# A linear-attention and mixture-of-experts kernel: attention in plain fp32 on halves of the matmul array, and expert units whose second layer lags and whose end is shared

## The chip, the cores and the metric

The kernel runs on one core of a Trainium2 chip. The metric is the device time of one launch in microseconds; lower is better. A core has a matmul engine (TensorE, PE in the profile, its weight loads PEld), a vector engine (VectorE, DVE), a scalar engine (ScalarE, ACT), GpSimd (POOL) and a synchronisation engine (SyncE, SP) that issues most of the transfers. PE writes into PSUM, 8 banks of 128 partitions x 512 fp32; everything else stands in SBUF or in device memory.

## The reference

Attention with exponential features, then one expert per token:

```
def phi(x):
    proj = einsum('bhsd,df->bhsf', x, w_phi)              # 64 -> 128
    proj = proj - max(abs(proj), axis=-1, keepdims=True)
    return concatenate([exp(proj), exp(-proj)], axis=-1)  # 256 features
q_p, k_p = phi(q), phi(k)
kv  = einsum('bhsf,bhsd->bhfd', k_p, v);  z = sum(k_p, axis=2)
attn = einsum('bhsf,bhfd->bhsd', q_p, kv) / (einsum('bhsf,bhf->bhs', q_p, z) + 1e-6)

x = attn as (4608, 512)
xn, en = x and expert_emb, each row divided by (its norm + 1e-6)
logits = xn @ en.T / tau;  expert = argmax(logits);  gate = softmax(logits)[expert]
out[token] = gate * (relu(x[token] @ w1[expert]) @ w2[expert])   # 512 -> 1024 -> 512
```

The shapes are 8 batches, 8 heads, 576 tokens and 64 columns a head; 8 experts; all arrays are fp32.

## The kernel before, in words

**Attention** goes through 16 quads: one quad is two pairs of heads (X = 0, 1; e = 0, 1 within a pair) of half a batch. `load` and `load_v` (L174, L182) bring q, k and v of a quad. Each of them is split into two float32r parts, the rounded value and what the rounding leaves: `split`, `split_v` and `split_k` (L208, L215, L244) do it with a copy on ACT or DVE (L203, L206) and a subtraction on DVE or POOL (L197). A product of two such pairs is three float32r matmuls, high by high, high by low and low by high.

A quad has nine blocks of 128 tokens in five groups (`GR`: 2, 2, 1, 2, 2 blocks). `proj` (L220) multiplies a group of q or k by the features: per block three matmuls at L229, 128 x 256 results for both heads of a pair at once, by a weight matrix that holds w_phi twice on its diagonal. Then DVE takes the largest absolute value of each row out of PSUM (L233) and subtracts it (L235). For keys, ACT makes the two exponentials (L242); for queries, PE transposes the blocks (`qtr`, L257) and ACT makes the exponentials from PSUM (L260). `kv` (L269) forms [v 1]^T k_p with 65 weight columns and 256 moving columns, three matmuls per block (L282), and ACT copies it (L285). `kve` (L287) turns it around on PE (L296), which also multiplies it with the experts' normalised embeddings, so that every head has 73 columns: 64 of kv, the sum, and 8 dots with the embeddings. DVE copies them (L298). `num` (L303) multiplies the queries' features by these in plain fp32 (L310, L313), and `norm` (L316) divides on DVE and writes x, and each fourth time sends x to device memory. `frame` (L844) writes out the order of a quad's work by hand, with the routing steps of earlier tokens put between (`pop`, `square`). On PE this order is kept; the other engines are ordered by a scheduler. The first quad is `first_frame` (L927), in written order on all engines but SP.

**Routing** (`route`, `early`, `tables`; L381, L466, L489) computes experts and gates on DVE and puts the tokens into a table by expert with indirect transfers of POOL. `tables` then makes a list of units: an expert's tokens in slots of 128, two slots to a unit; where the number of slots is odd, an expert has a first unit of three slots (the third may hold 32, 64 or 96 tokens), or a single one.

**Experts.** Unit 0 has three slots and begins before routing is through. Every later unit is a switch (L838) with 12 arms: 6 sizes, each with or without being an expert's last. Each arm holds the whole unit (`unit`, L799). In `layers` (L718) chunk c of the hidden features (128 of 1024) goes through layer 1: 12 matmuls (L688), weights w1 in halves, tokens moving; ACT makes the rounded part (L690) and DVE the rest (L693). Then comes layer 2 of chunk c - 1: per slot three matmuls with 512 moving columns (L711, L706). Layer 1 uses two PSUM banks in turn, and the hidden features three buffers. In an expert's last unit the next expert's weights are split chunk by chunk (`next_w1`, `next_w2`, L584). POOL gathers the rows of a unit two ahead (L604), DVE transposes the next unit's (L617), and ACT and DVE split them (`xsplit`, L641) into the one pair of buffers xh, xl. A unit of one slot has code of its own (`layers_of_slot`, L750), in which w1 moves (L765) and the hidden features are turned by PE (L774). A unit ends with ACT multiplying by the gate (L817) and POOL writing the rows out by an indirect transfer (L823).

## Time and profile before

| what | us |
|---|---|
| three runs, median (lowest to highest) | 1093.22 (1090.64 to 1102.72) |
| span of the one profiled execution, whose own time the page gives only as this span | 1133.1 |
| PE busy in it | 965.3 (85%) |
| DVE busy | 651.2 (57%) |
| POOL busy | 538.0 (47%) |
| ACT busy | 433.5 (38%) |
| mean granted PE clock | 0.908 of full speed |

The profiled execution is longer than the runs, and its rows add up to its own span. A row of instructions in order of time has the start, the duration, engine, line, operation, result<-operands and shape; in brackets the idle time ahead of it and what ended that. A row of groups has the count, the busy time, the mean duration in ns, and after the second bar the idle time ahead. Matmuls overlap: the time from one start to the next is the price of one, and its duration is longer. In "128\*64 128x73" the first pair is the weights' rows and columns, the second the moving operand. float32r shows as f32 there.

### The profile page before, as it was taken

How to read it: one execution, taken by the hardware profiler on the slowest of the kernel's cores; microseconds unless marked ns; L12 is line 12 of the kernel's file. 1: busy time of each engine (PE TensorE's matmuls, PEld its weight loads, DVE VectorE, ACT ScalarE, POOL GpSimd, SP SyncE). 2: the span in 40 equal slices, each digit the busy share in tenths (PEclk: the TensorE clock that was granted, in tenths of full speed). 3: DMA queues.
4: the chain of work that ended last, by engine and by line, in shares of the span. 5: the costliest groups of instructions: out<-in, count | busy, mean ns of one | idle time of the engine just before them, and what ended most of it. 6: DMA issues, size and time to landing. Idle time of an engine off the chain costs nothing. (4 is left out here: it accounts for less than half of the span.)

```text
span 1133.1 us, 17328 instructions
## 1 busy us (share of the span) xinstructions
PE 965.3 (85%) x6188; PEld 860.1 (76%) x6188; DVE 651.2 (57%) x1289; ACT 433.5 (38%) x841; POOL 538.0 (47%) x396
## 2 busy tenths in 40 slices
PE   6999999999899989988898788698687588798874
PEld 4899888888788878877787677587576477687763
DVE  8888898989899898969221223324225623422221
ACT  5556554645354554543221223314225413312221
POOL 5555564776477664655433224325144454422322
PEclk7999998999899999989899888799788778899887
DMA  5223221313132224111611111514313531511111
GB/s 166 83 66 106 61 88 46 105 51 106 63 105 66 79 90 180 45 29 43 215 37 49 38 40 49 191 23 126 106 45 116 159 123 46 188 28 45 47 35 43
DMA packets 55822, 94.22 MB, mean 83 GB/s; under 512 B 22471, under 2 KB 22855, under 8 KB 55440
## 3 DMA queue, kind: packets, MB, share of 16 engines
q1 hardware_dynamic: 45808, 68.97, 19.2%
q0 software_dynamic: 9632, 21.32, 6.3%
q14 instruction: 285, 2.33, 0.7%
q8 instruction: 97, 1.59, 0.7%
HBM read 70.64 MB, written 19.96 MB: 80 GB/s over the span
## 5 line engine op out<-in xcount | busy, mean ns | idle before, releaser
L604 POOL DMA_INDIRECT xg<-xd,ix x156 | 152.6, 978 | 260.2 <-DVE xt L617 168.5
L693 DVE SCALAR_TENSOR_TENSOR hl<-bk,hh 128x256 fp32r<-128x256 f32 (+2 forms) x128 | 57.6, 452 | 340.9 <-ACT hh L690 275.9
L197 POOL TENSOR_TENSOR kpl<-kp,kph 128x1024 fp32r<-128x1024 f32 (+1 forms) x79 | 170.1, 2153 | 121.3 <-DVE kph L206 111.7
L688 PE MATMUL bk<-xh,w1h 128*128 128x256 f32 (+4 forms) x512 | 169.5, 331 | 61.6 <-issue 54.2
L690 ACT ACTIVATE hh<-bk 128x256 fp32r<-128x256 f32 (+4 forms) x128 | 52.6, 415 | 346.4 <-PE bk L688 248.7
L688 PEld LDWEIGHTS bk<-xh,w1h 128*128 128x128 f32 x512 | 111.2, 217 | 73.4 <-issue 60.7
L688 PE MATMUL bk<-xl,w1h 128*128 128x256 f32 (+4 forms) x512 | 166.6, 325 | 0.0
L688 PE MATMUL bk<-xh,w1l 128*128 128x256 f32 (+4 forms) x512 | 165.9, 324 | 0.0
L260 ACT ACTIVATE qp<-bk 128x512 f32<-128x512 f32 (+1 forms) x160 | 79.9, 552 | 148.0 <-PE bk L257 134.5
L310 PE MATMUL np<-kvs,qp 128*128 128x73 f32 x992 | 126.1, 283 | 0.0
L310 PEld LDWEIGHTS np<-kvs,qp 128*128 128x128 f32 x992 | 124.2, 203 | 0.1
L688 PEld LDWEIGHTS bk<-xl,w1h 128*128 128x128 f32 x512 | 111.7, 218 | 4.9
L233 DVE TENSOR_REDUCE m<-bk 128x4 f32<-128x512 f32 (+1 forms) x157 | 98.9, 632 | 28.4 <-PE bk L229 22.6
L206 DVE CAST kph<-kp 128x1024 fp32r<-128x1024 f32 (+1 forms) x77 | 109.7, 1424 | 6.6 <-ACT kp L242 6.1
L688 PEld LDWEIGHTS bk<-xh,w1l 128*128 128x128 f32 x512 | 110.9, 217 | 0.0
L242 ACT ACTIVATE kp<-kd 128x512 f32<-128x512 f32 (+1 forms) x160 | 83.6, 580 | 50.2 <-DVE kd L235 49.5
L823 POOL DMA_INDIRECT out<-o,ent x39 | 41.0, 1052 | 95.5 <-ACT o L817 88.6
L711 PE MATMUL bk<-w2h,hh 128*128 128x512 f32 x136 | 59.7, 439 | 31.2 <-ACT hh L690 23.2
L711 PE MATMUL np<-w2h,hl 128*128 128x512 f32 (+1 forms) x160 | 65.7, 411 | 0.0
L711 PE MATMUL np<-w2h,hh 128*128 128x512 f32 (+1 forms) x160 | 65.4, 409 | 0.0
L711 PE MATMUL np<-w2l,hh 128*128 128x512 f32 (+1 forms) x160 | 65.2, 408 | 0.0
L257 PE MATMUL bk<-cst,qd 128*128 128x128 f32 x288 | 50.3, 296 | 8.9 <-DVE qd L235 8.9
(248 smaller groups left out, 2210.6 us busy)
## 6 DMA issues: line engine op xcount, KB each, us to landing
w1r<-w SPq DMA_DIRECT2D x14, 1024.0 KB
w2r<-w SPq DMA_DIRECT2D x14, 1024.0 KB
q<-qT SPq DMA_DIRECT2D x16, 576.0 KB
k<-kT SPq DMA_DIRECT2D x15, 576.0 KB
xd<-x SPq DMA_DIRECT2D x8, 1024.0 KB
va<-va SPq DMA_DIRECT2D x16, 325.0 KB
va<-va SPq DMA_DIRECT2D x16, 260.0 KB
xg<-xd,ix POOLq DMA_INDIRECT x156
```

Of the source, the lines that this page charges most:

```text
L197: ins = eng.tensor_tensor(out=hl[1], in0=raw, in1=hl[0].bitcast(F32), op=ALU.subtract)
L206: self.v.tensor_copy(out=out, in_=in_)
L233: v.tensor_reduce(out=m, in_=pv, axis=AX.X, op=ALU.max, apply_absolute_value=True)
L242: nc.scalar.activation(out=k[:, :nu, s], in_=d[:, :nu], func=AF.Exp, scale=sc)
L257: nc.tensor.transpose(out=ps[:, e, c, :], in_=self.dq[g][:, c, e, :], identity=self.ident)
L260: nc.scalar.activation(out=q[:, s, :, :nu], in_=ps[:, :, :nu], func=AF.Exp, scale=sc)
L310: nc.tensor.matmul(out=n[:, i * W:(i + 1) * W], lhsT=self.qp[g][:, s, e, c], rhs=self.kvs[j][:, X, e, s], start=(s == 0), stop=(s == 1))
L604: ins = nc.gpsimd.indirect_dma_start(out=self.xg[i][:, q * P:(q + 1) * P], out_offset=None, in_=self.xd.rearrange("n (g d) -> (n g) d", g= ...
L688: nc.tensor.matmul(out=ps, lhsT=w[:, d, fs], rhs=x[:, d, :n], start=(d == 0 and i == 0), stop=(d == 3 and i == 2))
L690: high = nc.scalar.activation(out=hh[:, :n], in_=ps, func=AF.Relu)
L693: low = self.v.scalar_tensor_tensor(out=out, in0=ps[:, cs], scalar=0.0, in1=hh[:, cs].bitcast(F32), op0=ALU.max, op1=ALU.subtract)
L711: self.nc.tensor.matmul(out=self.acc[a // P][:b - a], lhsT=h[:, a:b], rhs=w[:, c], start=(c == 0 and i == 0), stop=(c == 7 and i == 2))
```

## The change

- **Plain fp32 instead of three float32r products.** All splits of q, k, v and of the keys' features are gone, with their buffers. `proj` multiplies each head by itself: 64 weight rows (a head's columns) at partitions 0 to 63 or 64 to 127, 128 moving columns, one matmul per block and head; the two heads' results go to the two banks of one PSUM pair, one pair for keys and one for queries.
- **kv already turned.** `kv` takes the keys' features as weights, 64 columns at a time, and [v 1 and the dots of v with the embeddings] as 73 moving columns; the result has features on the partitions, and `kve` is gone. The dots of v are made ahead by the new `vemb` from a second, transposed copy of v (vT), 8 moving columns each, and put beside v by ACT. v's array now has 10 blocks, padded by zeros, so that no block is shared.
- **num on halves.** `num` splits each block's 128 weight columns into two of 64, which write to partitions 0 to 63 and 64 to 127.
- **Five slots per quad.** The order of PE is no longer `frame` but `slot`: in each of 83 slots one group of keys, one of queries two slots later, its transposes one slot later, a quarter of kv at lag 4, and num at lags 7 and 8.
- **Experts.** The one-slot code is gone, and there are 14 arms: 2 x 7 of size, first unit of an expert, and last. Layer 2 lags layer 1 by five chunks; layer 1 uses five banks in turn, and there are eight buffers of hidden features and two pairs of token buffers. Layer 2 of the last three chunks of the first two slots, and their outputs, stand once behind the switch for all arms (`unit_end`). There the next unit's arm is read into registers and named to the engines ahead of those matmuls (`switch_hint`). The second half of w2 is split in the next expert's first unit. Instructions of one element (`idle`) give all arms the same counts. The units' order is as written on all engines.

On PE, in the steady piece of attention before (L229 proj, L310 and L313 num):

```order
L229 MATMUL bk_64<-wph,kh 128x256
L229 MATMUL bk_64<-wpl,kh 128x256
L229 MATMUL bk_64<-wph,kl 128x256
L310 MATMUL np<-kvs,qp 128x73 x8
L313 MATMUL np<-kvs,qp 64x73 x2
```

And a slot and a half of the steady piece now (L231 transposes, L243 vemb, L265 kv, L213 proj, L284 and L287 num; PE):

```order
L231 MATMUL bk_65<-cst,qd 128x128 x4
L243 MATMUL pj_63<-et,vt 128x8 x4
L265 MATMUL bk_66<-va,kp_848 64x73 x4
L265 MATMUL bk_66<-va,kp_898 64x73 x4
L265 MATMUL bk_66<-va,kp_771 64x73 x2
L265 MATMUL bk_66<-va,kp_848 64x73 x4
L265 MATMUL bk_66<-va,kp_898 64x73 x4
L265 MATMUL bk_66<-va,kp_771 64x73 x2
L213 MATMUL pj_63<-wp,kt 128x128 x2
L213 MATMUL pj_64<-wp,qt 128x128 x4
L284 MATMUL np<-kvs,qp 64x73 x16
L287 MATMUL np<-kvs,qp 64x73 x2
```

A projection of one block was three matmuls and is two, num of a head was eight of 128 rows of results and is sixteen of 64, and every row but L231 and L287 now consists of pairs on two halves.

On PE, the end of unit 0 and the switch to unit 1 before (L711 layer 2, L838 the switch, L765 the first arm):

```order
L711 MATMUL np<-w2h,hh_5534 128x512
L711 MATMUL np<-w2l,hh_5534 128x512
L711 MATMUL np<-w2h,hl_5537 128x512
L132 TENSOR_LOAD tab
L1085 SWITCH_STRIDE
L1085 ISA x2
L838 BRANCH_PREFETCH_HINT
L765 MATMUL bk_63<-w1h,xh 128x512
```

The same place now has two pieces, the first within layer 2 (L691) of unit 0, between its fifth chunk and its sixth, where the arm is read (PE):

```order
L691 MATMUL acc_5697<-w2h,qp 128x512
L691 MATMUL acc_5697<-w2l,qp 128x512
L691 MATMUL acc_5697<-w2h,qp 128x512
L140 TENSOR_LOAD tab
L714 SWITCH_STRIDE
L714 ISA
L714 BRANCH_PREFETCH_HINT
L691 MATMUL bk_66<-w2h,qp 128x512
L691 MATMUL bk_66<-w2l,qp 128x512
```

and the second, PE again, at the switch itself, 27 matmuls of layer 2 and 12 transposes later (L669 layer 1 of unit 1):

```order
L691 MATMUL acc_5697<-w2l,qp 128x512
L691 MATMUL acc_5697<-w2h,qp 128x512
L998 SWITCH_STRIDE
L998 ISA x2
L833 BRANCH_PREFETCH_HINT
L669 MATMUL pj_64<-x,w1h 128x256 x2
```

The load of the arm's number and a hint moved from directly ahead of the switch to a place with matmuls between; in later units these are the 18 of the shared end.

The core of the diff:

```diff
-NK = 5
-AT = 3, 5
-ST = 1, 3, 4
+LAG, CUT = 5, 5
+ARMS = [(k, first, last) for k, first in ((256, 0), (256, 1), (384, 1), (352, 1), (320, 1), (288, 1), (128, 1)) for last in (0, 1)]
+NB = 10
...
     def proj(self, j, n, g):
-        h, l = self.half[n]
-        self.turn += 1
-        ps = self.banks[self.turn % len(self.banks)].rearrange("p (c e f) -> p c e f", c=2, e=2)
+        ps = self.pj[1 - n][:, :, :nu]
         for c in range(nu):
             us = slice((u0 + c) * P, (u0 + c + 1) * P)
-            for i, (a, b) in enumerate(((h, self.wh), (h, self.wl), (l, self.wh))):
-                nc.tensor.matmul(out=ps[:, c].rearrange("p e f -> p (e f)"), lhsT=a[:, us], rhs=b,
-                                 start=(i == 0), stop=(i == 2))
+            for e in range(2):
+                r = slice(HD * e, HD * e + HD)
+                nc.tensor.matmul(out=ps[:, e, c], lhsT=self.raw[j, n][r, us], rhs=self.wp[r], start=True, stop=True)
...
+    def vemb(self, j, b0):
+        t = self.raw[j, 2]
+        ps = self.bk[0][:, 3 * P:], self.bk[1][:, 3 * P:]
+        for b in range(b0, b0 + 2):
+            for e in range(2):
+                r = slice(HD * e, HD * e + HD)
+                self.nc.tensor.matmul(out=ps[e][:, b * E:(b + 1) * E], lhsT=t[r, b * P:(b + 1) * P],
+                                      rhs=self.et[r, 2 * (j % 2) + b // 5], start=True, stop=True)
+        if b0 == NB - 2:
+            for e in range(2):
+                self.nc.scalar.copy(out=self.va[j][:, :, e, HD + 1:], in_=ps[e][:, :NB * E].rearrange("p (b x) -> p b x", x=E))
...
     def kv(self, j, X, e):
-            for n, (a, b) in enumerate(((vh, kh), (vl, kh), (vh, kl))):
-                nc.tensor.matmul(out=o, lhsT=a[r, u, e], rhs=b[r, c, :, e], start=(i == 0 and n == 0), stop=(i == 4 and n == 2))
+        for s in range(2):
+            c0 = (2 * e + s) * W
+            for i in range(5):
+                g, c, u = self.where(X, i) if i < 4 else (2, 0, 4)
+                for a in (0, 64):
+                    nc.tensor.matmul(out=self.bk[5][a:a + 64, c0:c0 + W], lhsT=self.kp[g][:, s, e, c, a:a + 64],
+                                     rhs=self.va[j][:, 5 * X + i, e], start=(i == 0), stop=(i == 4))
...
     def num(self, j, X, e):
             for s in range(2):
-                nc.tensor.matmul(out=n[:, i * W:(i + 1) * W], lhsT=self.qp[g][:, s, e, c], rhs=self.kvs[j][:, X, e, s],
-                                 start=(s == 0), stop=(s == 1))
+                for a in (0, 64):
+                    nc.tensor.matmul(out=n[a:a + 64, i * W:(i + 1) * W], lhsT=self.qp[g][:, s, e, c, a:a + 64], rhs=kvs[:, s],
+                                     start=(s == 0), stop=(s == 1))
...
+    def layers(self, t, n, first, e):
+        nxt = t + 1 < NU
+        slots = range(-(-n // P))
+        for c in range(8 + CUT):
+            if c < 8:
+                self.layer1(t, c, n, (8 * t + c) % 5)
+                if e is not None:
+                    self.next_w1(c, e)
...
+                if first and 1 <= c < 5:
+                    self.wsplit(1, c + 3)
...
+            if c == LAG and nxt:
+                self.ahead(t)
+            if c == 8 and nxt:
+                if e is not None:
+                    self.turned([2])
...
+                self.xtr(t + 1, 2 + (e is not None))
+            if LAG <= c < LAG + CUT:
+                self.layer2(c - LAG, n, slots)
...
+        for c in range(CUT, 8):
+            self.layer2(c, n, slots[2:])
+        if n > 2 * P:
+            self.output(t, n, 2)
...
+    def unit_end(self, t):
+        if t + 1 < NU:
+            self.arms[t + 1] = self.arm(t + 1)
+            self.tc.switch_hint(self.arms[t + 1], len(ARMS), label=f"unit{t + 1}")
+        self.done = []
+        for i in range(2):
+            for c in range(CUT, 8):
+                self.layer2(c, 2 * P, [i])
+            self.output(t, 2 * P, i)
...
-            for arm in self.tc.Switch({e: self.reg(t, 1, [e], 0, 11) for e in ENGINES}, 12):
-                self.unit(t, (P, 2 * P, 3 * P, 3 * P - 32, 3 * P - 64, 3 * P - 96)[arm // 2], arm % 2)
+            for arm in self.tc.Switch(self.arms[t], len(ARMS), hint=f"unit{t}"):
+                self.unit(t, *ARMS[arm])
+            self.unit_end(t)
             self.units(t + 1)
...
+    def slot(self, t):
+        j, r = at(-2)
+        if r is not None and j > 0:
+            self.vemb(j, 2 * r)
+        j, r = at(4, 4)
+        if j is not None:
+            self.kv(j, r // 2, r % 2)
+        j, r = at(8, 3)
+        if r in (0, 2) and not (j == NQ - 1):
+            self.num(j, r // 2, 1 - r // 2)
...
+            self.proj(j, 1, r)
+        self.square()
+        j, r = at(2)
...
+            self.proj(j, 0, r)
...
+        j, r = at(7, 4)
+        if j is not None and r in (0, 3) and not (j == NQ - 1):
+            self.num(j, r // 3, r // 3)
...
+        j, r = at(3)
+        if r is not None and not (j == NQ - 1 and r == 4):
+            self.qtr(j, r)
```

Here `at(lag)` gives the quad and the slot in it that lie `lag` slots back.

More of the change, by code (lines that the diff above doesn't have):

```diff
@@ L454, in scatter @@
                 in_=ent[:, t, :], in_offset=None)
-            for split in (self.last, self.last_k):
-                self.after(ins, split, mybir.DependencyClass.NoSync, "the splits are waited for")
             for other in self.scat:
@@ L831, in units, with first_unit, arm @@
+    def first_unit(self, extra):
+        self.done = []
+        self.first_layers(K * P, extra)
+        for i in range(K):
+            self.output(0, K * P, i)
+        self.gather_parts(2, range(2))
+    def arm(self, t):
+        return {e: self.reg(t, 1, [e], 0, len(ARMS) - 1) for e in ENGINES}
     def units(self, t):
@@ L1053, in rest @@
                 self.tables()
+                for c in range(4, 8):
+                    self.wsplit(1, c)
                 while self.sends:
```

570 lines of the change are left out of this document (201 added, 369 removed).

## The prediction

> **What bounds the kernel now.** I read the page's totals and slices first, then the busy times by stage, then the costliest groups of each stage, then the instructions in order of time at two places. The page:
>
> ```profile
> span 1133.1 us, 17328 instructions
> PE 965.3 (85%) x6188; PEld 860.1 (76%) x6188; DVE 651.2 (57%) x1289; ACT 433.5 (38%) x841; POOL 538.0 (47%) x396
> PE   6999999999899989988898788698687588798874
> DVE  8888898989899898969221223324225623422221
> PEclk7999998999899999989899888799788778899887
> ```
>
> The columns show two programs: up to slice 19 both PE and DVE are near full, after it DVE is nearly idle and PE has holes in which its clock sags. So the two are priced apart, from the table of busy times by stage (start and end, length, PE busy, PEld, DVE, ACT, POOL, granted clock, DMA share, GB/s):
>
> ```profile
> 60.00:500.00 440.00, 412.20 (x3249) 377.57 (x3247) 390.74 (x736) 226.83 (x438) 269.11 (x146) 0.97 0.26 82
> 510.10:560.50 50.40, 43.60 (x239) 38.89 (x237) 31.63 (x131) 15.51 (x34) 24.03 (x22) 0.96 0.34 109
> 560.50:1118.80 558.30, 451.65 (x2320) 393.03 (x2320) 172.74 (x327) 155.13 (x307) 206.40 (x203) 0.87 0.27 80
> 1118.80:1133.10 14.30, 0.38 (x1) 0.00 (x0) 0.00 (x0) 0.69 (x1) 2.03 (x2) 0.62 0.15 47
> ```
>
> They are a steady piece of attention, the first expert unit, units 1 to 16, and a tail without work. In attention PE is busy 94% and DVE 89%: either alone would hold the stage. The DVE groups there:
>
> ```profile
> L206 DVE CAST kph<-kp 128x1024 fp32r<-128x1024 f32 (+1 forms) x70 | 99.7, 1425 | 5.9 <-ACT kp L242 5.4
> L233 DVE TENSOR_REDUCE m<-bk 128x4 f32<-128x512 f32 (+1 forms) x141 | 88.5, 630 | 20.8 <-PE bk L229 19.9
> L197 DVE TENSOR_TENSOR ql<-q,qh 128x1152 fp32r<-128x1152 f32 x14 | 30.6, 2188 | 0.0
> L298 DVE COPY kvs<-bk 128x292 f32<-128x292 f32 x29 | 13.1, 451 | 0.5 <-PE bk L296 0.5
> L235 DVE TENSOR_TENSOR qd<-bk,m 128x512 f32<-128x512 f32 (+1 forms) x71 | 44.9, 632 | 1.1
> ```
>
> There are 70 key groups, five to a quad, so 14 quads in 440 us: **31.4 us a quad**. All of attention ends at 510.1.
>
> **Attention, DVE.** Removed are the three groups L206, L197 and L298: 99.7 + 30.6 + 13.1 = 143.4 us. What stays is 390.7 - 143.4 = 247.3 us, or 17.7 us a quad. ACT keeps its ten exponentials a side and loses the splits, POOL loses the subtractions; neither is the bound even now (226.8 and 269.1 us of 440).
>
> **Attention, PE.** The groups of num (L310, L313) in the same stage, shapes kept apart:
>
> ```profile
> L310 PE MATMUL np<-kvs,qp 128*128 128x73 f32 x903 | 115.5, 284 | 0.0
> L313 PE MATMUL np<-kvs,qp 128*64 128x73 f32 x228 | 27.9, 246 | 0.0
> ```
>
> In 14 quads these are 64 and 16 records a quad, where the code writes 32 and 8 matmuls: a plain fp32 matmul is two records. Their prices, in order of time:
>
> ```profile
> 510.14 1.53 PE L677 MATMUL bk<-cst,xt 128*128 128x128 f32 x12
> 511.51 1.90 PE L310 MATMUL bk<-kvs,qp 128*128 128x73 f32 x16
> 513.34 0.47 PE L313 MATMUL bk<-kvs,qp 128*64 128x73 f32 x4
> 513.74 2.01 PE L310 MATMUL bk<-kvs,qp 128*128 128x73 f32 x16
> ...
> 232.06 0.28 PE L282 MATMUL bk<-kph,v0l 128*65 128x256 f32 x1
> 232.18 0.28 PE L282 MATMUL bk<-kpl,v0h 128*65 128x256 f32 x1
> 232.39 0.33 PE L282 MATMUL bk<-kph,v1h 64*65 64x256 f32 x1
> ```
>
> Starts give the price: sixteen records with 128 weight columns take 1.83 us, 0.114 each, and a transpose (L677) also 0.114. Four with 64 weight columns last 0.47; less one record's length (0.246 above), three steps take 0.22: 0.07 each. A change of the piece of the array in use costs 0.21 instead of 0.12, so 0.09.
>
> A quad has after the change: kv 80 matmuls with 64 weight columns (160 records), num 72 (144 records, 128 of them in pairs), projections 36 with 64 weight rows (72 records), vemb 20 (40 records), 18 transposes, and some 25 changes of shape. One after the other this is 11.2 + 10.1 + 8.2 + 4.6 + 2.1 + 2.3 = **38.5 us**. If two halves run at once, the pairs cost half: 5.6 + 5.6 + 4.1 + 2.3 + 2.1 + 2.3 = **22.0 us**. The trace of before never uses two halves side by side, so these are the two ends of the unknown price. I take the lower: the halves differ in rows, or in columns and in output partitions, and PEld already runs beside PE (377.6 us of loads within the 412.2 of matmuls). With PE at 22.0, DVE at 17.7 and one PSUM pair each for queries and keys, I allow PE 92% busy, as it is now: **24 us a quad**. Sixteen quads and about 16 us of start and end make 400, against 510.1: **-110 us**.
>
> Taken away with the splits is cover: the first projections wait for raw loads alone. A quad now loads 2.58 MB instead of 1.78; in 24 us that is 108 GB/s, against 82 now at a DMA share of 0.26. I put it at nothing. SP has its loads a quad ahead, v's only two slots (about 9 us); were these late, vemb, at the head of PE's slot, would stall, and with it everything behind it on PE.
>
> **Units.** An ordinary unit's end, PE in order of time, and the rate in a long unit:
>
> ```profile
> 655.90 0.39 PE L711 MATMUL np<-w2h,hl 128*128 128x512 f32 x1
> 657.65 0.50 PE L711 MATMUL bk<-w2h,hh 128*128 128x512 f32 x1 [1.36 <-ACT hh L690]
> 658.91 0.40 PE L711 MATMUL np<-w2h,hl 128*128 128x512 f32 x1
> 663.61 0.55 PE L688 MATMUL bk<-xh,w1h 128*128 128x256 f32 x1 [4.30 <-issue]
> 663.97 0.42 PE L688 MATMUL bk<-xl,w1h 128*128 128x256 f32 x1
> 664.18 0.41 PE L688 MATMUL bk<-xh,w1l 128*128 128x256 f32 x1
> ...
> 1015.35 0.34 PE L688 MATMUL bk<-xh,w1l 128*128 128x384 f32 x1
> 1015.52 0.39 PE L711 MATMUL bk<-w2h,hh 128*128 128x512 f32 x1
> 1015.75 0.40 PE L711 MATMUL bk<-w2l,hh 128*128 128x512 f32 x1
> ```
>
> ```profile
> 632.36:663.58 31.22, 25.59 (x144) 22.68 (x144) 7.18 (x15) 6.60 (x14) 9.65 (x10) 0.88 0.15 41
> ```
>
> 384 columns take 0.17 us and 512 take 0.23, so 0.45 ns a column: 0.12 for 256. A unit of 256 tokens is 96 x 0.12 + 48 x 0.23 = 22.6 us of matmuls, but lasts 31.2: 8.6 lost. Of these 1.4 wait for ACT's hidden features, 4.3 pass at the switch, and the next 24 matmuls run at 0.21 instead of 0.12 (2.2). The shapes of the units:
>
> ```profile
> L688 PE MATMUL bk<-xh,w1h 128*128 128x256 f32 x320 | 101.2, 316 | 39.2 <-issue 39.2
> L688 PE MATMUL bk<-xh,w1h 128*128 128x352 f32 x64 | 23.7, 370 | 6.4 <-issue 6.4
> L688 PE MATMUL bk<-xh,w1h 128*128 128x384 f32 x64 | 22.9, 359 | 4.2 <-issue 4.2
> L688 PE MATMUL bk<-xh,w1h 128*128 128x320 f32 x32 | 11.1, 347 | 7.4 <-ACT xh L203 7.4
> L688 PE MATMUL bk<-xh,w1h 128*128 128x288 f32 x32 | 10.6, 331 | 4.4 <-issue 4.4
> L765 PE MATMUL bk<-w1h,xh 128*128 128x512 f32 x8 | 3.8, 469 | 4.0 <-issue 4.0
> ```
>
> A unit has 32 of the first kind: ten of 256, two of 352, one of 384 beside unit 0, one each of 320, 288 and 128. By the same rate 10 x 22.6 + 2 x 32.3 + 33.7 + 29.0 + 27.6 + 19.1 = **400 us**; the 128-token unit (L765 now) becomes 96 loads at 0.11 and 36 matmuls at 0.23. They last 558.3 now, so 9.9 us a unit is lost.
>
> With a lag of five, hidden features are needed five chunks of layer 1 after PE has left their bank to ACT and DVE, so the 1.4 us goes. At the switch PE has 12 matmuls of the arm (2.8 us) and 18 of the shared end (4.2 us) to run while its sequencer loads the register, jumps and fetches; before, nothing. ACT and DVE, which come later through the same switch, have five banks (7 us) of grace. The loss left lies between 0 (all covered) and 8.6 (nothing covered). The price at the switch, 4.3, is under the 7.0 of cover, so I lean to the low end: 2.5 us a unit for units in which gathers or splits come late. 400 + 16 x 2.5 = 440: **-118 us**. The new waits: the next unit's tokens are split on ACT and DVE behind the eighth hidden chunk; DVE's transposes of the third slot stand ahead of them and wait for POOL's gathers, and behind them stands the next unit's first matmul, 8 us of PE work later.
>
> **Unit 0** is 50.4 us with 33.7 of matmuls (as 384 above). The chain of routing on DVE and the gather of unit 1's tokens is not shortened, so only the switch and its slow start go: **-5 us**. The tail of 14.3 stays.
>
> **Sum:** 1133.1 - 110 - 118 - 5 = 900 us of span. The profiled span stands to the runs' median as 1133.1 to 1093.2, a factor of 0.965, so **868 us**.
>
> **Rivals.**
>
> *Only some of the overlap* (0.10). If row halves overlap and column halves don't, a quad is 11.2 + 10.1 + 4.1 + 2.3 + 2.1 + 2.3 = 32.1, at 96% busy 33.4 us: 150 more, 1013 us. If weight loads take turns as now, about 36 us a quad and 1054. For it: PEld is 377.6 of 440 us already. Against: a load runs during a matmul everywhere.
>
> The Trainium skill, "TensorE: Matmul & The Clock Gate", Part 3, says that matmuls on different tiles run at once (three column tiles gained 2.38x), but that a load overlaps a running matmul only where row groups differ. By that rule kv and num, whose halves share all rows, would go as in this rival; PEld beside PE with all rows in use speaks against so strict a reading here.
>
> *No overlap at all* (0.06): 38.5 us, PE always busy, 39.7 a quad: 251 more, 1111 us, 1.6% slower; half of this chance goes to no change, since it lies at the edge. *Every change of half drains* (0.03): 208 matmuls x 0.09 more, 57 us a quad, 528 more, about 1378 us: slower. The point from which attention decides so is 900 + 16 x (q - 24) = 1133, q = 38.6 us a quad. For it: the rows at 232.18 and 232.39, where a new shape cost 0.09. Against: those change the size of the piece, here only its place changes.
>
> *The single PSUM pair sets the pace* (0.11): DVE orders reduce, reduce, subtract, subtract, each 0.63 by its row, and the next keys' projection waits for the third, behind a normalisation at times. At 30 us a quad 96 more: 961 us. Against: 2.5 us of other matmuls stand between.
>
> *The shared end covers nothing* (0.13), the change not doing what it says: the jump into the end and the register's load come before the 18 matmuls, and the queue runs dry there. 4.3 + 2.2 + 1 a unit, 520 instead of 440: 946 us.
>
> *Issue sets attention's pace* (0.03): no record may start sooner after another than some floor, however small it is. The smallest records of this trace are these eight, 0.6 us in all with 0.2 for the last one, so 0.057 apart:
>
> ```profile
> L168 PE MATMUL bk<-cst,x 8*64 8x8 f32 x8 | 0.6, 199 | 4.2 <-DVE x L165 4.2
> ```
>
> The change has 434 records a quad; at 0.057 these are 24.7, at 95% busy 26.0 us a quad, 32 more: 899 us. Against: the eight also load 64 columns each, so their spacing need not be a floor.
>
> The Trainium skill, "TensorE: Matmul & The Clock Gate", section "Wait — 56ns, not 53.3ns?", states such a floor of about 62 ns per matmul for the case that the hardware decode is off; by it a quad would be 26.9 us of issue and the time about 935 us, but the eight records came faster.
>
> **How the numbers follow.** The forecast has 0.54; its own range, from 21.5 to 26.5 us a quad and 0.9 to 4.4 lost a unit, is 805 to 936. A measurement tells about 1% from no change. Faster by over 1%: 0.54 + 0.10 + 0.11 + 0.13 + 0.03 = 0.91; within 1%: 0.03; slower: 0.03 + 0.03 = 0.06. The range of 790 to 1020 takes in all but the tails of the forecast, the worse half of the first rival and the slow ones, about 0.18.
>
> **What would show it.** Right: about 24 us from one quad to the next; 16 records of num (L284) in 0.6 us, not 1.1; no CAST on DVE in attention; units of 256 tokens about 25 us apart; PE idle under 2 us at a switch and its clock near 1.0 throughout. Wrong: matmuls of one pair starting 0.07 or more apart; a quad of 30 us with PE waiting on DVE; gaps of 4 us at switches.

## The result, and the profile after

The changed kernel takes **1015.3 us** (median of 4 runs, 1009.2 to 1031.7) where the kernel before takes 1094.4 beside it: a ratio of 0.925, 95% interval 0.918 to 0.932. It is faster, as forecast, but by 79 us where 226 were predicted. The profiled execution has a span of 1009.5 us and took 1011.4, so here the two hardly differ. The kernel before took 1094 to 1100 us in some of the sets of runs that follow (the quicker ones) and 1135 to 1145 in others (the slower ones), so times are compared within a set, and ratios across sets only with care.

The same rows of the page as those shown of before:

```profile
span 1009.5 us, 24334 instructions
PE 848.5 (84%) x9556; PEld 752.9 (75%) x9556; DVE 487.7 (48%) x1312; ACT 389.4 (39%) x909; POOL 280.3 (28%) x261
PE   6888978888888888876899998798689689879996
DVE  3555566556565566567422334434336443622332
PEclk9998899989998999999999999999899579989998
```

VectorE has fallen from 57% to 48%, but TensorE is mostly at 8 tenths in attention, where it stood mostly at 9. The stages, by the table of busy times (length, PE, PEld, DVE, ACT, POOL, granted clock, DMA share, GB/s): a steady piece of attention, unit 0, units 1 to 16, the tail.

```profile
60.00:400.00 340.00, 290.11 (x5385) 258.84 (x5382) 201.46 (x506) 155.63 (x356) 23.12 (x21) 0.94 0.36 118
452.40:507.80 55.40, 42.77 (x268) 37.34 (x269) 33.23 (x130) 15.48 (x33) 21.19 (x22) 0.97 0.25 76
507.80:999.80 492.00, 426.49 (x2397) 377.62 (x2395) 190.09 (x487) 168.78 (x414) 207.84 (x189) 0.94 0.31 92
999.80:1009.50 9.70, 0.00 (x0) 0.00 (x0) 0.00 (x0) 0.69 (x1) 2.02 (x2) 0.66 0.21 68
```

Against the terms of the sum: attention ends at 452.4 (400 was expected), unit 0 takes 55.4 (45), units 1 to 16 take 492.0 (440), the tail 9.7 (14.3). Neither engine is the bound in attention: PE 85% busy, DVE 59%.

**Attention.** Where PE's time goes shows in PE's order of time over one slot; the second fence is VectorE in the same 4 us:

```profile
153.80 0.72 PE L213 MATMUL pj<-wp,kt 64*128 64x128 f32 x8
154.34 0.61 PE L213 MATMUL pj<-wp,qt 64*128 64x128 f32 x8
154.89 0.66 PE L231 MATMUL bk<-cst,qd 128*128 128x128 f32 x4
157.28 0.61 PE L243 MATMUL pj<-et,vt 64*128 64x8 f32 x8 [1.74 <-DVE kd L217]
157.83 1.49 PE L265 MATMUL bk<-va,kp 128*64 128x73 f32 x40
159.25 0.72 PE L213 MATMUL pj<-wp,kt 64*128 64x128 f32 x8
...
163.55 1.19 PE L284 MATMUL np<-kvs,qp 128*64 128x73 f32 x32
164.57 0.42 PE L287 MATMUL np<-kvs,qp 128*64 128x73 f32 x4
```

```profile
154.57 0.67 DVE L316 TENSOR_TENSOR x<-np,rec 128x512 f32<-128x512 f32 x1
...
155.36 1.27 DVE L215 TENSOR_REDUCE m<-pj 128x4 f32<-128x512 f32 x2
156.56 0.67 DVE L217 TENSOR_TENSOR kd<-pj,m 128x512 f32<-128x512 f32 x1
```

The overlap is there: kv's 40 records take 1.42 us from 157.83 to the next line's start, num's 32 take 1.02, so 0.032 to 0.036 each. Read record by record, they start in pairs, the two of a pair 0.006 to 0.007 us apart, with a pair about every 0.063 us (157.943 and 157.950, then 158.007 and 158.013). But the value embedding (L243), first in its slot, starts at 157.28, just as the subtraction of the keys ends (156.56 + 0.67). Its output stands in the upper columns of the two banks that hold the projected keys. VectorE was busy with a normalisation, then with both reductions. Behind the waiting L243 stand kv and num, which have nothing of VectorE to wait for here. The waits of PE in this window, in total, with their number and the longest:

```profile
PE pj L243 <- DVE kd L217: 46.5, 37, 2.7
```

That is nearly all of the 49.9 us in which PE is idle there.

**Units.** The switches are covered: before, PE idled there 54 us in 14 gaps of up to 4.6 us; now it is 7 us in fifteen, 1.8 us at most. The loss sits inside. An ordinary unit starts at 542.57, and after 24 matmuls this is seen on all engines:

```profile
545.19 0.42 DVE L674 SCALAR_TENSOR_TENSOR hl<-pj,hh 128x256 fp32r<-128x256 f32 x1 [10.85 <-ACT hh L671]
545.28 0.28 PE L669 MATMUL pj<-xh,w1l 128*128 128x256 f32 x1
545.65 0.38 ACT L671 ACTIVATE hh<-pj 128x256 fp32r<-128x256 f32 x1 [0.56 <-PE pj L669]
546.07 0.42 DVE L674 SCALAR_TENSOR_TENSOR hl<-pj,hh 128x256 fp32r<-128x256 f32 x1 [0.45 <-ACT hh L671]
546.55 0.38 PE L669 MATMUL pj<-xh,w1h 128*128 128x256 f32 x1 [0.99 <-DVE hl L674]
```

The third chunk has a bank of its own, bank 3, free since the unit before. It starts at 546.55, when VectorE has read the second chunk out of bank 2. Banks 2 and 3 are one tile, `pj1`. Behind a switch that takes ScalarE and VectorE long, the same wait is longer:

```profile
649.90 0.32 PE L669 MATMUL pj<-xh,w1l 128*128 128x352 f32 x1
654.35 0.43 PE L669 MATMUL pj<-xh,w1h 128*128 128x352 f32 x1 [4.14 <-DVE hl L674]
```

```profile
646.06 0.68 ACT L784 ACTIVATE o<-acc,ent 128x512 f32<-128x512 f32 x1
651.75 0.46 ACT L671 ACTIVATE hh<-pj 128x352 fp32r<-128x352 f32 x1 [5.00 <-issue]
```

ScalarE needs 5 us for the switch, and PE, after three chunks, finds bank 1 held by the reading of bank 0. Over 500 to 1009 us:

```profile
PE pj L669 <- DVE hl L674: 37.1, 17, 7.0
PE pj L669 <- DVE qp L674: 14.0, 13, 1.3
PE pj L669 <- DVE hh L674: 7.2, 2, 6.0
```

Every one of these 58 us is a wait on a tile `pj`; on the single-bank tile `bk` there is none for VectorE. Two waits of 1.0 us are those of an ordinary unit; the long ones, 3 to 7 us, stand behind slow switches.

### The profile page after: what moved, and what is told of

Read it like the earlier page. It is cut to its first block, busy times and chain, and to the rows that moved or that the text cites. A ratio compares the mean times of both kernels' runs of the same rounds, so it can differ in the third digit from the quotient of the medians.

```text
span 1009.5 us, 24334 instructions
## 1 busy us (share of the span) xinstructions
PE 848.5 (84%) x9556; PEld 752.9 (75%) x9556; DVE 487.7 (48%) x1312; ACT 389.4 (39%) x909; POOL 280.3 (28%) x261
## 4 chain that ended last, share of the span: by engine, by line
PE 61%; DVE 19%; issue 9%; ACT 7%; DMA 2%; POOL 1%; ACTq 1%; SPq 0%; DVEq 0%; POOLq 0%
PE pj L669 17%; PE acc L691 9%; PE bk L265 8%; PE bk L691 6%; PE np L284 6%; DVE m L215 5%; PE pj L213 5%; PE pj L243 4%; PE bk L669 4%; DVE kd L217 3%; DVE x L316 2%; PE bk L231 2%; PE np L287 1%; DVE hl L674 1%; ACT sq L338 1%
## 5 line engine op out<-in xcount | busy, mean ns | idle before, releaser
L215 DVE TENSOR_REDUCE m<-pj 128x4 f32<-128x512 f32 (+1 forms) x160 | 98.3, 632 | 142.4 <-PE pj L213 134.7
L669 PE MATMUL pj<-xh,w1h 128*128 128x256 f32 (+4 forms) x236 | 77.1, 327 | 44.1 <-DVE hl L674 23.6
L669 PE MATMUL pj<-x,w1h 128*128 128x256 f32 (+3 forms) x408 | 89.0, 314 | 28.3 <-DVE hl L674 17.8
L265 PE MATMUL bk<-va,kp 128*64 128x73 f32 x2560 | 106.1, 243 | 0.4
L243 PEld LDWEIGHTS pj<-et,vt 64*128 64x128 f32 x640 | 46.2, 205 | 71.6 <-DVE kd L217 66.0
L243 PE MATMUL pj<-et,vt 64*128 64x8 f32 x640 | 53.2, 272 | 54.5 <-DVE kd L217 53.7
L265 PEld LDWEIGHTS bk<-va,kp 128*64 128x64 f32 x2560 | 95.7, 148 | 2.7 <-issue 0.8
L669 PEld LDWEIGHTS pj<-x,w1h 128*128 128x128 f32 x408 | 70.1, 200 | 34.5 <-DVE hl L674 19.8
L669 PEld LDWEIGHTS pj<-xh,w1h 128*128 128x128 f32 x236 | 49.6, 210 | 51.7 <-DVE hl L674 25.9
L284 PE MATMUL np<-kvs,qp 128*64 128x73 f32 x1984 | 76.8, 230 | 0.0
L691 PE MATMUL acc<-w2h,qp 128*128 128x512 f32 (+2 forms) x216 | 75.1, 390 | 0.0
L669 PE MATMUL pj<-xl,w1h 128*128 128x256 f32 (+4 forms) x236 | 74.6, 316 | 0.0
L669 PE MATMUL pj<-xh,w1l 128*128 128x256 f32 (+4 forms) x236 | 74.4, 315 | 0.0
L213 PE MATMUL pj<-wp,kt 64*128 64x128 f32 x576 | 60.0, 328 | 14.1 <-DVE kd L217 5.1
```

Source lines behind the costliest of these rows:

```text
L213: nc.tensor.matmul(out=ps[:, e, c], lhsT=self.raw[j, n][r, us], rhs=self.wp[r], start=True, stop=True)
L215: v.tensor_reduce(out=m, in_=ps, axis=AX.X, op=ALU.max, apply_absolute_value=True)
L243: self.nc.tensor.matmul(out=ps[e][:, b * E:(b + 1) * E], lhsT=t[r, b * P:(b + 1) * P], rhs=self.et[r, 2 * (j % 2) + b // 5], start=True, s ...
L265: nc.tensor.matmul(out=self.bk[5][a:a + 64, c0:c0 + W], lhsT=self.kp[g][:, s, e, c, a:a + 64], rhs=self.va[j][:, 5 * X + i, e], start=(i = ...
L284: nc.tensor.matmul(out=n[a:a + 64, i * W:(i + 1) * W], lhsT=self.qp[g][:, s, e, c, a:a + 64], rhs=kvs[:, s], start=(s == 0), stop=(s == 1))
L669: nc.tensor.matmul(out=ps, lhsT=w[:, d, fs], rhs=x[:, d, :n], start=(d == 0 and i == 0), stop=(d == 3 and i == 2))
```

## The experiments

The kernels sent together, a set, ran on one chip, each with the kernel before beside it, and ratios are to that. In the edited kernels line numbers lie up to four higher.

**1. The kernel before, a second profile.**

> The kernel before, unchanged, for a second profile. The prediction scaled its span by 1093.2/1133.1. If the long span of the first profile was an outlier of that execution, this profile has a span of 1089 to 1105 us with attention ending near 495 to 510 and the units 15 to 40 us shorter. If profiling itself lengthens this kernel, the span is again about 1130.

It spans 1141.0 us, in a set where its runs take 1139 (median). So profiling adds nothing that shows: most likely the 1133.1 us span of the first profile belongs to such conditions, and the 1093 us runs to others. The prediction's factor of 0.965 joined the two.

**2. Single banks.** Behind attention the two two-bank tiles are given up, and their four banks are declared again as four tiles of one bank. (Number 8 has this edit again, in one set with the other.)

```diff
-        pj = [ps.tile([P, 2, 512], F32, name=f"pj{i}") for i in range(2)]
+        b45 = [ps.tile([P, 512], F32, name=f"bk{i}") for i in (4, 5)]
+        self.close_np = ExitStack()
+        ps = self.close_np.enter_context(tc.tile_pool(name="pjp", bufs=1, space=PSUM))
+        pj = [ps.tile([P, 2, 512], F32, name=f"pj{i}") for i in range(2)]
...
+            self.bk[:4] = [pool.tile([P, 512], F32, name=f"bk{i}") for i in range(4)]
             self.acc = [self.bk[5]] + [pool.tile([P, 512], F32, name=f"acc{i}") for i in range(1, 3)]
```

> The changed kernel, but after attention the four banks of the two projection pairs are declared as four tiles of one bank each instead of two tiles of two. Theory A: in the units a first layer's matmul waits for VectorE's read of the other bank of its pair (two waits of about 1.15 us in an ordinary unit, up to 7 us after a switch), because the pair is one tile. Then the 58 us of PE waits for VectorE's lower halves in the units fall under 15 us, the first 72 matmuls of an ordinary unit take 8.6 us instead of 10.9, and the time falls by 40 to 60 us to 955 to 975. Rival B: the passage of ScalarE and VectorE through the switch (about 9 us without VectorE work) is too long for any five banks, and the stalls only move from the third or fourth chunk to the sixth: a fall of 15 us at most, 1000 or more.

980.8 us, a ratio of 0.861 (0.854 to 0.869) in the slower set. By the ratio theory A holds, rival B falls, and the gain is larger than expected: ordinary units start 22.2 to 22.5 us apart, which is the 22.6 of dense matmuls, and their first 72 matmuls take 8.5 us instead of 10.9. The waits of PE for VectorE in the units, 58 us in the change, are 3 us.

**3. The value embedding behind the keys' projection**, first try: its call moved behind that of the projection, which in program order is also behind VectorE's reduction and subtraction.

```diff
-        j, r = at(-2)
-        if r is not None and j > 0:
-            self.vemb(j, 2 * r)
...
             self.proj(j, 1, r)
+        j, r = at(-2)
+        if r is not None and j > 0:
+            self.vemb(j, 2 * r)
```

> The changed kernel, but the value-embedding matmuls stand behind the keys' projection of their slot instead of at the head of the slot. Theory A: at the head they wait for VectorE's subtraction of the keys of the slot before (46.5 us in 340 us of attention), and hold up kv and num which need not wait; moved, a quad takes about 25 us instead of 27 and the time falls by 20 to 40 us to 975 to 995. Rival C: the keys' projection, which writes the same banks, then waits as long, since PE and VectorE take turns anyway: 1005 to 1020.

1192.8 us, slower than the kernel before (1139.3). The edit did the opposite of what was meant: the matmuls now wait for the reading of the keys that have just been projected, in every slot. Over the same 60 to 400 us as above:

```profile
PE pj L243 <- DVE kd L217: 90.4, 46, 8.8
```

A quad takes 33 to 45 us. It is a doubling of the suspected wait, and shows what such a wait costs at the head of TensorE's queue.

**4. Keys first on VectorE**: the queries' reduction goes behind the keys' subtraction (`self.keys`) in the engine's order.

```diff
-        v.tensor_reduce(out=m, in_=ps, axis=AX.X, op=ALU.max, apply_absolute_value=True)
+        top = v.tensor_reduce(out=m, in_=ps, axis=AX.X, op=ALU.max, apply_absolute_value=True)
+        if n == 0 and self.keys is not None:
+            self.after(top, self.keys, mybir.DependencyClass.NoSync, "the keys' banks first")
```

> The changed kernel, but VectorE reduces and subtracts the keys before it reduces the queries (before: both reductions, then both subtractions). Theory A: the keys' banks come free 0.5 to 0.6 us earlier in each of 80 slots and the value-embedding matmuls, which wait for that, start so much earlier: 20 to 45 us less, 970 to 995. Rival C: PE then waits as much at the queries' banks or at ScalarE: 1005 to 1020.

A ratio of 0.928 (0.921 to 0.935), no difference from the change. The wait is 38.1 us of 340 in this slower set, where the change has 48.0 in another slower one (number 8). Releasing the banks 0.6 us sooner is not enough; the theory's number for this edit was wrong.

**5. The change itself, and both edits.** In the second try the value embedding stands between the keys' matmuls and VectorE's reduction of them:

```diff
-    def proj(self, j, n, g):
+    def proj(self, j, n, g, values=(None, None)):
...
+        if values[0]:
+            self.vemb(values[0], 2 * values[1])
         m = self.pa.tile([P, 2, 2], F32, name="m", bufs=4)[:, :, :nu]
...
-        j, r = at(-2)
-        if r is not None and j > 0:
-            self.vemb(j, 2 * r)
...
-            self.proj(j, 1, r)
+            self.proj(j, 1, r, at(-2))
```

> The changed kernel, unchanged, beside the others of this call. Its ratio to before should again be 0.92 to 0.93. In the kernels with single banks and with the keys first (but not in the first profile of the change) three quads of attention took 34 us instead of 27, where nine scatters of the routing stood in a row on GpSimd and TensorE sat at issue. If that comes with the chip, it shows here too where this call runs on such a chip; if it comes with the edits, this profile has no quad over 30 us.

> Single banks for the units, and the value-embedding matmuls between the keys' projection and VectorE's reduction of it (so that they wait for no reading of the keys of their own that the projection has not waited for already). Theory A: the 46 us of waits at the slots' heads go, a quad takes 24.5 to 25.5 us instead of 27, attention ends 25 to 40 us earlier, and the ratio to before falls from 0.861 to 0.83 to 0.84. Rival C: the wait stands at the keys' projection instead, a quad stays at 26.5 to 27.5 and the ratio at 0.855 to 0.865.

The control took 1021.9 us, 0.932 (0.924 to 0.941), with no quad over 31.5. Both edits: **852.2 us, 0.776 (0.768 to 0.783)**, far more than theory A expected for the second edit. PE in order of time, over one slot:

```profile
155.79 1.49 PE L269 MATMUL bk<-va,kp 128*64 128x73 f32 x40
157.12 1.19 PE L288 MATMUL np<-kvs,qp 128*64 128x73 f32 x32
158.14 0.42 PE L291 MATMUL np<-kvs,qp 128*64 128x73 f32 x4
158.49 0.71 PE L215 MATMUL pj<-wp,kt 64*128 64x128 f32 x8
159.03 0.51 PE L247 MATMUL pj<-et,vt 64*128 64x8 f32 x8
159.40 0.69 PE L215 MATMUL pj<-wp,qt 64*128 64x128 f32 x8
```

In this slot no wait is left. Over 60 to 360 us the keys' projection, which now has kv and num in front of it, still waits for the keys' subtraction nine times, 7.8 us in all, 0.9 at most; that is what remains of the single PSUM pair. The lengths of quads 2 to 9, from the first copy of kvs in one quad to that in the next, in the change and with both edits:

```
change  27.3 29.2 26.2 26.9 27.2 29.2 26.2 26.9
both    21.2 22.0 22.2 22.1 23.5 22.0 22.2 22.1
```

22.0 is the sum that the prediction made of PE's work in a quad. The stages show a nearly full PE and a nearly full clock, too (a piece of attention, units 1 to 16):

```profile
60.00:360.00 300.00, 283.51 (x5730) 255.65 (x5724) 217.04 (x570) 166.23 (x389) 44.54 (x41) 0.99 0.44 148
429.40:844.70 415.30, 408.35 (x2397) 366.39 (x2395) 184.38 (x487) 166.18 (x414) 205.47 (x187) 0.97 0.35 109
```

**6. The halves in turn.** kv and num run one half's matmuls, then the other's; the edit exchanges two loops:

```diff
-            for i in range(5):
-                g, c, u = self.where(X, i) if i < 4 else (2, 0, 4)
-                for a in (0, 64):
+            for a in (0, 64):
+                for i in range(5):
+                    g, c, u = self.where(X, i) if i < 4 else (2, 0, 4)
```

> The changed kernel, but kv and num run all matmuls of the first 64 columns and then all of the second 64, instead of the two halves by turns; the work is the same. If the overlap of the halves is what the quad's 0.033 us a record comes from, these records are 0.064 to 0.07 apart, kv's 40 take 2.6 to 2.8 us instead of 1.4 and num's 32 take 2.1 instead of 1.08, a quad is 7 to 10 us longer (34 to 37) and the time 110 to 160 us longer, about 1120 to 1180. Rival: records of 64 columns take 0.033 anyway, and nothing changes.

1080.0 us in its one execution, 58 more than the control in its set. kv, and what follows it:

```profile
199.77 2.17 PE L265 MATMUL bk<-va,kp 128*64 128x73 f32 x40
201.86 0.49 PE L213 MATMUL pj<-wp,kt 64*128 64x128 f32 x4
```

2.09 us for 40 records, 0.052 each on the mean instead of 0.035. Read record by record, the matmuls of one half start 0.063 us apart (199.881, 199.944, 200.007, 200.071, 200.137, 200.200), which is nearly the 0.064 to 0.07 expected; only where the order passes from one half to the other do some of both run side by side (200.200 and 200.206), and this brings the mean down. So the alternation is what gives the overlap. Its worth is 60 us here and not 110 to 160: some of the overlap was left, and PE's wait for VectorE gave back 8 us of 340 (38.7 instead of 46.6 in the control).

**7. The scatters of the routing spread.** In the slower sets three quads of the changed kernel and its variants take 7 to 11 us more than the others. In the edit the scatters of one routing wait for VectorE's subtractions, two at a time.

```diff
                 in_=ent[:, t, :], in_offset=None)
+            if T == 9:
+                self.after(ins, self.shift, mybir.DependencyClass.Sync, "two in a slot")
```

> As single banks with the value embedding moved, and the routing's scatters of attention wait for VectorE's subtractions, so that at most two follow one another on GpSimd instead of nine. Theory D: nine indirect transfers in a row starve TensorE's supply of instructions (four records, then 1.1 us of nothing); spread, three quads lose up to 7 us each less, and the ratio falls by another 0.01 to 0.02 where the control shows such quads. Rival: each scatter costs the same 0.8 us wherever it stands, and the time stays.

> Both edits and the routing's scatters spread (at most two behind one another), as measured before beside a kernel before of 1096 us, where nothing was to be gained because no quad was slow. Theory D: on a chip where the kernel before takes about 1137 us and three quads take 32.4 us with both edits, these three fall to 22 to 26 us, 20 to 30 us in all, a ratio near 0.775. Rival: each scatter holds TensorE's instructions up by the same 1 us wherever it stands: the slots with scatters stay long, 0.795 to 0.80. Where the kernel before takes 1095, nothing: 0.775 to 0.785.

> Both edits alone, on the same chip, for comparison: 0.776 where the kernel before takes about 1095, 0.797 where it takes about 1140.

0.780 (0.773 to 0.787) in the set of number 5, and 0.783 (0.774 to 0.792) beside 0.777 (0.768 to 0.786) without the edit in a last set. Both times the kernel before took 1096 to 1100, so there was no slow quad to mend, and nothing follows but that the edit gains nothing there.

**8. The four corners**, on one chip, in a slower set.

> The changed kernel with its two-bank tiles kept everywhere, and only the value-embedding matmuls moved between the keys' projection and VectorE's reduction. If the two causes are independent, attention is that of the kernel with both edits (quads of 22.2 us) and the units are those of the change (ordinary units of 24.6 us): the ratio to before is 0.93 less about 16 x 5 = 80 us less the slots' better clock, 0.84 to 0.86. If the gain of the two together came from the banks, it is 0.91 or more.

> The changed kernel, unchanged, as the first corner of four on one chip. Where the kernel before takes about 1095 here, 1015 to 1022; where it takes about 1137, the three quads behind the scatters take 34 us and it is 1050 to 1065.

> Single banks alone, the second corner. Theory A, two causes in two stages, each with its own price: 55 to 75 us less than the first corner.

> The value embedding moved alone, the third corner. Theory A: 75 to 100 us less than the first corner (16 quads by 4.7 to 5, and a quicker end of attention).

> Both, the fourth corner. If the two add, its distance from the first corner is the sum of the two others within 15 us, 130 to 175 us, and with them the whole miss of the prediction is accounted for (1015 to 868 is 147). If they share a cause (the granted clock, which sags with every wait), the sum of the single edits is smaller than the two together by 30 us or more.

Kernel before 1144.6 us. Stages in us, from the first matmuls of each:

| kernel | time | ratio (95%) | attention ends | unit 0 | units 1-16 | tail |
|---|---|---|---|---|---|---|
| change | 1067.2 | 0.933 (0.926 to 0.940) | 478.7 | 56.3 | 520.3 | 10.1 |
| single banks | 986.2 | 0.867 (0.859 to 0.875) | 487.9 | 47.6 | 431.0 | 10.7 |
| embedding moved | 1004.2 | 0.878 (0.870 to 0.885) | 416.1 | 60.2 | 516.9 | 9.7 |
| both | 911.3 | 0.797 (0.791 to 0.803) | 413.1 | 51.4 | 440.5 | 11.4 |

Alone they gain 81 and 63 us, 144 together; both gain 156. So they add, within the 15 us expected, each in its stage: the banks take 76 to 89 us from the units, the embedding 63 to 75 from attention, and neither changes the other's stage by more than 10 us. The single gains were not as expected (81 for 55 to 75, 63 for 75 to 100). (The embedding alone, in an earlier set, had 0.882, 0.876 to 0.888, where 0.84 to 0.86 had been expected.) The waits of PE in the units, of the change and with single banks, the two largest of each:

```profile
PE pj L669 <- DVE hl L674: 46.4, 16, 6.9
PE pj L669 <- DVE qp L674: 13.2, 11, 2.2
```

```profile
PE bk L671 <- issue: 10.4, 12, 2.5
PE bk L671 <- ACT xh L200: 4.9, 1, 4.9
```

**9. What covers the switch.** Both on top of the two edits, in a slower set (kernel before 1135.1 us). First, the register load and the hint behind the shared end instead of ahead of it.

```diff
-        if t + 1 < NU:
-            self.arms[t + 1] = self.arm(t + 1)
-            self.tc.switch_hint(self.arms[t + 1], len(ARMS), label=f"unit{t + 1}")
         self.done = []
         for i in range(2):
             for c in range(CUT, 8):
                 self.layer2(c, 2 * P, [i])
             self.output(t, 2 * P, i)
+        if t + 1 < NU:
+            self.arms[t + 1] = self.arm(t + 1)
+            self.tc.switch_hint(self.arms[t + 1], len(ARMS), label=f"unit{t + 1}")
```

> Single banks and the value embedding moved, and in the units' shared end the next arm's register load and the hint of the switch come behind its 18 matmuls and its outputs instead of ahead of them. If those matmuls are what covers TensorE's passage through the switch, the gap from the last matmul of a unit to the first of the next goes from 0 to 1.5 us to 3.5 to 5, and the time rises by 50 to 90 us, to a ratio of 0.82 to 0.86. Rival (the prediction's third on the units: the end covers nothing): no change, 0.77 to 0.78.

Then, layer 2 one chunk behind layer 1 instead of five (the splits that follow layer 2 move with it):

```diff
-            if LAG <= c < LAG + CUT:
-                self.layer2(c - LAG, n, slots)
+            if 1 <= c < 1 + CUT:
+                self.layer2(c - 1, n, slots)
```

> Single banks and the value embedding moved, and in units 1 to 16 the second layer lags one chunk behind the first instead of five (the split at chunk five and the shared end stay). If the lag is what took away the waits for ScalarE's hidden features, each unit waits 1 to 3 us more for its first chunks, above all behind a switch, where ScalarE and VectorE come 5 to 9 us late: 16 x 2 to 5 us, 30 to 80 us more, a ratio of 0.80 to 0.85. Rival: five single banks cover it, and the lag is worth under 10 us: 0.775 to 0.785.

The load last: 913.8 us, 0.801 (0.794 to 0.807), against 0.797 (0.791 to 0.803) for both edits alone in the next set: no difference that these intervals show, some 5 us in the middle, where 50 to 90 were expected. But the edit did not take the cover away: TensorE's sequencer reaches the moved load when the first of the 18 matmuls starts (517.27 and 517.25 in one ordinary unit), and the last of them ends at 521.49, so they still run while it loads and switches. The gaps at the fifteen switches are 17 us in this profile, 4.3 at most, where both edits alone have 4 in the next set. So the place of the load costs little time, and what the 18 matmuls cover is not settled by this run.

The lag of one: 964.2 us (950.1 to 973.4), 0.848 (0.839 to 0.856). That is 50 us more than the load last in the same set, and 0.051 x 1135 = 58 us more than both edits alone by the ratios, as expected. Its gaps at the fifteen switches are 19 us, about those of the load last, so what it adds stands elsewhere: PE waits again for hidden features.

```profile
PE bk L695 <- ACT hh L675: 15.9, 9, 3.6
```

The lag is the part of the units' change that these runs show to carry weight.

**10. 128 tokens as 256.** In the table of arms 128 is replaced by 256; the second slot holds padding, whose rows go nowhere.

```diff
-ARMS = [(k, first, last) for k, first in ((256, 0), (256, 1), (384, 1), (352, 1), (320, 1), (288, 1), (128, 1)) for last in (0, 1)]
+ARMS = [(k, first, last) for k, first in ((256, 0), (256, 1), (384, 1), (352, 1), (320, 1), (288, 1), (256, 1)) for last in (0, 1)]
```

> Single banks and the value embedding moved, and the unit of 128 tokens runs as one of 256, its second slot filled with the table's padding: more work, 96 matmuls of 256 columns in place of 96 of 128. If matmuls of 128 columns, each with a load of 128 columns, are what took the granted clock to 0.50 in that unit (32 us for 19 us of matmuls), the clock stays near 1.0, the unit takes 23 to 24 us and the time falls by 7 to 10 us, to a ratio of 0.766 to 0.772. Rival: the throttle answers to something else in this place (the routing of transfers, the switch before it), the unit keeps half the clock and takes 40 us or more: 0.782 or more.

0.802 (0.797 to 0.807) in the set of number 9: no gain. From start to start the unit takes 32.0 us; with 128 columns it took 30.1 in this set (load last). The busy times of the unit, as 128 with both edits (number 5), as 128 with the scatters spread (the last set of number 7), and as 256 up to its last matmuls:

```profile
660.20:692.00 31.80, 30.51 (x132) 27.84 (x132) 17.36 (x36) 15.48 (x33) 15.07 (x15) 0.62 0.56 184
```

```profile
662.70:688.40 25.70, 22.10 (x132) 19.82 (x132) 15.86 (x34) 14.71 (x32) 14.49 (x12) 0.87 0.70 214
```

```profile
708.40:738.00 29.60, 26.22 (x144) 23.31 (x144) 20.09 (x39) 17.76 (x36) 13.15 (x13) 0.88 0.55 187
```

The clock with 256 columns is 0.88 on the mean. With 128 it was 0.62 in one profile and 0.87 in another, so this run does not show that the shape has to do with it.

## Why the prediction was wrong, and where it was right

**The direction and the overlap were right.** Two halves of the array run at once (0.032 to 0.036 us a record, loads included), VectorE's casts are gone, the lag covers the hidden features, and TensorE's queue, with its work and its one wait, sets a quad. Of the rivals, some of the overlap, no overlap, the drain and the issue floor are refuted by those records. That 1015 still lies between 790 and 1020 is luck: none of the rivals for which that range was made so wide came about as described.

The Trainium skill, "TensorE: Matmul & The Clock Gate", Part 3, lists that a weight load overlaps a running matmul only where row groups differ, though the text above that list also names a background weight buffer. The measurement differs from the list: kv's and num's halves share all 128 rows, and with a load for every record they ran 0.032 to 0.036 apart by turns, 0.063 within one half.

**Attention: the step that failed is "with PE at 22.0, DVE at 17.7 and one PSUM pair each for queries and keys, I allow PE 92% busy".** The 22.0 was right to a few per cent; a quad takes that in the kernel with the embedding moved, with PE 94% busy. Term by term it was less exact (eight records of the projection take 0.54 us, from 153.80 to 154.34, where the sum has 0.46), and the errors cancel in part. The 92% is not what the table of before has, which is 94%, but that is under 1 us a quad. The change stands at 27 us and 85% because the value embedding heads TensorE's queue and writes into the keys' banks. The prediction did name vemb "at the head of PE's slot" as what would stall, but only for late loads, and the rival of the single PSUM pair put the wait at the keys' projection, with 2.5 us of other matmuls in front. In the trace these matmuls stand behind the wait. Price: 52 us of attention in the first profile; when it is moved, 63 us come back in a slower set, and with both edits attention ends at 378.4 in the quicker one, 74 us sooner. This wait is a real one: its output shares a bank with what VectorE reads. The Trainium skill, "PSUM — Partial Sum Buffer", section "Terms", says that TensorE writing and VectorE reading the same bank and quadrant at once is an error; no run here tried that, and the runs only show that the order was kept.

**Units: the step that failed is "ACT and DVE, which come later through the same switch, have five banks (7 us) of grace".** Four of the five banks are two tiles, and TensorE waits for a tile: two waits of 1.0 us in an ordinary unit, 3 to 7 us behind a slow switch. With four tiles in their place the same matmuls run without them, and the units lose (415.3 - 400) / 16 = 1.0 us each in the quicker set, where 2.5 were allowed. The diff showed it: the banks became views of `pj`. I counted banks, not tiles. Price: 52 us of units and some of unit 0's 10.

**The other 38 us are the scale.** The sum in spans was 900 and the profiled execution had 1009.5, 110 of the 147 us. The factor of 0.965, taken from a profile of before whose 1133 us the second one finds again only in a slower set, took another 32 off, and the median lies 6 above that execution's span. Like for like the account is simpler: in a slower set the change spans 1065.4 us, 165 above the sum's 900, and both edits take 149 of these away (916.4). That both edits reach 852 in the quicker set, near the forecast of 868, therefore owes something to the wrong factor. A smaller term was off too: the unit of 128 tokens, put at 19.1 us, took 41.0 in the change and 32 without the false waits, most of it at half the clock.

**The shared end's matmuls as cover** was right in its effect (7 us of gaps at the switches instead of 54). Its reason was not tested: where the load stands behind these matmuls, the sequencer still reaches it while they run, and no run leaves them out. That the lag leaves TensorE's queue free of waits, so that its sequencer is at the switch early, fits both runs; it was not shown by itself. What holds TensorE up in the three long quads of the slower sets stays open as well.

## What to carry to other kernels

Count the waits by tile, not by bank: two banks made into one tile, so that one instruction can read both, turn into one thing to wait for wherever they are then used singly. Before an operation is put at the head of an in-order queue, ask which bank it writes and who still reads there; here 0.6 us of work a slot, at the wrong place, made 27 us of a quad of 22. And a factor between a profile and a median is worth nothing when the two may come from different conditions.

## What the runs showed of the hardware

**Half the clock with TensorE busy.** In the unit of 128 tokens the granted clock goes to 0.50 for 7 to 31 us in all profiles of the change and its edits that run it with 128 columns. With both edits (number 5) PE is busy throughout (30.5 of the 31.8 us shown in number 10), and its matmuls start 0.21 us apart instead of the 0.11 of its first sixteen. How long it lasts differs between executions: 24, 14 and 7 us in three profiles from quicker sets, with both edits in numbers 5 and 7 and with the scatters spread in the last set, in which the unit took 32.0, 28.2 and 25.7 us. The Trainium skill, "TensorE: Matmul & The Clock Gate", Part 1, ties the half clock to an idle window; with both edits PE's longest idle time just ahead is 1.2 us, so the page's rule does not cover this case. The cause was not isolated.

**TensorE starved beside scatters.** In the slower sets, nine indirect transfers in a row on GpSimd, 1.28 us apart, go with TensorE at "issue": four records, then 0.9 us of nothing. TensorE in such a stretch of the kernel with both edits, then GpSimd:

```profile
163.20 0.51 PE L288 MATMUL np<-kvs,qp 128*64 128x73 f32 x4 [0.93 <-issue]
164.63 0.54 PE L288 MATMUL np<-kvs,qp 128*64 128x73 f32 x5 [0.91 <-issue]
```

```profile
162.38 0.97 POOL L430 DMA_INDIRECT tbl<-ents,r_adr  x1 [0.30 <-issue]
163.65 0.97 POOL L430 DMA_INDIRECT tbl<-ents,r_adr  x1 [0.31 <-issue]
```

The same stretch of the same kernel in the quicker set, with its nine scatters as far apart, has 236 records of PE in 11.5 us instead of 86. That the two go together is seen in three places of each slower profile read, of the change and its edits with the halves by turns. That the scatters cause it was only argued: they alone are not enough, and PE's bursts come 1.43 us apart and do not keep step with them. The clock has a share in the long quads, too. In each of these three places of the kernel with both edits it then stands at 0.50 for 13.7 us, and in the quicker set it does not. The first of them:

```profile
160.80:174.50 13.70, 9.73 (x97) 8.24 (x97) 2.67 (x4) 1.55 (x3) 3.88 (x4) 0.51 0.02 2
```
